# Where x is turned for the second block: TensorE transposes instead of DMA transposes, and a reordered prologue, in a linear-attention and feed-forward kernel

## The chip, the core and the metric

The kernel runs on one NeuronCore of a Trainium2 chip. The metric is the device time of one execution in microseconds (us). The core has five engines that run side by side and meet at semaphores: TensorE (PE, with its weight loads shown as PEld), VectorE (DVE), ScalarE (ACT), GpSimd (POOL) and SyncE (SP). DMAs are issued from POOL (bulk loads and stores) and from SP (a few loads, and all DMA transposes); both kinds move through the same 16 DMA engines.

## What is computed

The reference is a linear attention with cosine-weighted features, followed by a feed-forward layer with a quick GELU:

```
r = max(x, 0);  phi(x) = concat(r * cos_w, r * sin_w)        # x = q or k, weights depend on the position
kv  = einsum('bhsf,bhsd->bhfd', phi(k), v);   z = sum over s of phi(k)
att = einsum('bhsf,bhfd->bhsd', phi(q), kv) / (einsum('bhsf,bhf->bhs', phi(q), z) + 1e-6)
x   = att with heads put side by side                         # (8*576, 512)
h   = x @ w_in;  g = h * sigmoid(1.702 * h);  out = g @ w_out # w_in (512, 2048), w_out (2048, 512)
```

There are 8 batches, 8 heads, 576 positions and 64 values per head, so x has 4608 rows. All matrix products run in bf16 and accumulate in f32.

## The kernel before

**Two tilings that do not match.** Attention goes by batch: 576 rows, cut into four chunks of 128 and a tail of 64 (chunk 4). The feed-forward layer goes by blocks of `TB = 512` rows of x, nine in all. Block 1 is rows 512 to 1023: the tail of batch 0, chunks 0 to 2 of batch 1, and the first 64 rows of chunk 3 of batch 1. The tail of batch 1 (rows 1088 to 1151) is first read by block 2.

**One attention batch.** `prep` makes the features of q (`qn`) or k (`kp`) of one chunk with two DVE instructions; `prep_v` copies v into `vt`, which has a column of ones. The features of q are transposed into `qT`, by a DMA issued from SP (`turn_q`), or by eight TensorE transposes and a DVE copy (`turn_q_at`). `unit_kv` makes kv of all heads with 40 small matmuls, and two copies bring it to `kvs`. `unit_num(b, c)` multiplies a chunk with kv (8 matmuls of 65 columns into an `at` tile of PSUM) and divides on DVE: `den`, `inv`, then `xb`, the chunk of x. At last x has to be transposed into `xT`: `turn_x` does this with a DMA transpose from SP, `turn_x_at` with four TensorE transposes into an `at` tile and a copy on ACT. There are two `at` tiles, used in turn, and four `mm` tiles of one bank each.

**One block.** `mm1(i, fc)` takes 4 matmuls of 512 columns (line 249) and a GELU on ACT for each of the 16 slices of the hidden layer. `mm2` takes 64 matmuls (line 284) with `w_out` and empties the result through ACT or DVE to an output DMA. In block 0 the second product goes by parts: in slots 16 to 31 each slot does four matmuls for one of four row groups (`n % 4`), part 0 first, so that `w_out` is needed piece by piece.

**Order.** Nothing is scheduled automatically: each engine runs its instructions in the order of the program. While block `i` runs, the attention of batch `i + 1` is mixed in: the block has 32 slots, and `at(n, f, ...)` hangs a piece of work behind slot `n`. In block 0 batch 1 is worked on in slots 14 to 31: `prep` of q at 14, `turn_q_at` at 16 to 20, `prep` of k from 21, v at 24, `unit_kv` at 25, `unit_num` of chunks 0 to 4 at 26 to 30. Chunks 2 and 3 are turned by `turn_x_at` in slots 30 and 31; chunks 0, 1 and 4 by `turn_x`, whose DMA is issued from SP once DVE has written the chunk. From block 1 on all turns are DMA transposes.

**The prologue.** Batch 0 has nothing to hide behind, so it is written out by hand (lines 359 to 406): 34 matmuls on zeros while the first loads run; `prep` of k, then of q; `turn_q0`, transposes of q with a copy on ACT or DVE; `kv_half` for heads 0 to 3 and 4 to 7; `num0(n, p)` and `product0(n, p)` for half the heads and half the rows; `turn_x0(n, p)`, transposes of x into the tile `tp` with a copy on ACT. `mm1_first` does the first product of block 0 for three slices at once, in three pieces: over the first half of x's columns for all rows, then over the second half for rows 0 to 255, then for rows 256 to 511. The tail of batch 0's q is prepared last on DVE and transposed by DMA into `qT_tail` (line 404, line 189); `unit_num(0, 4)` reads it behind slot 7 of block 0. SP then issues three f32 loads of batch 1's tails, which stand behind that transpose in SP's queue.

**Loads.** POOL issues, in order, q and v of batch 0, `w_in`, the tail of q, then `w_out` and batch 1 in turn. From the ninth on each of them waits for the one eight places before it.

Of the kernel before, what the change touches and what calls it, by code (L numbers as in the profile page):

```python
# [21 lines left out]
def kernel(  # L22
# [15 lines left out]
    TB = 512  # L38
# [14 lines left out]
    def rows(c):  # L53
        return 128 if c < 4 else 64
# [4 lines left out]
    def mm_tile():  # L59
        return ps.tile([128, TB], F32, name="mm", bufs=4)  # L60
# [13 lines left out]
    def load_main(b, n, h0=0, h1=H, on=nc.gpsimd):  # L74
        if h0 == 0:
            state[b][n] = two.tile([128, 2048], BF16, name=n)
        on.dma_start(out=state[b][n][:, 256 * h0:256 * h1].rearrange("p (h e) -> p h e", h=h1 - h0),  # L77
                     in_=SRC[n][b, h0:h1, 0:512, :].rearrange("h (p c) d -> p h (c d)", c=4))
# [20 lines left out]
    def load_w_in(g, k0=0, k1=KC):  # L99
        nc.gpsimd.dma_start(out=w_in_sb[:, k0:k1, ts(g, 512)], in_=win_r[:, k0:k1, ts(g, 512)])  # L100

    def load_w_out(g):
        nc.gpsimd.dma_start(out=w_out_sb[:, ts(g, 4), :], in_=wout_r[:, ts(g, 4), :])
# [17 lines left out]
    load_tail(0, "q")  # L121
    for g in range(1, 4):
        load_w_in(g)
    load_w_out(0)
    load_main(1, "q")
    load_main(1, "k")
    load_w_out(1)
    load_main(1, "v")
# [34 lines left out]
    def part(b, n, c, h0, h1):  # L163
        if c == 4:
            return state[b][n, 4].rearrange("p (h d) -> p h d", d=D)[:, h0:h1]
        return state[b][n].rearrange("p (h c d) -> p c h d", c=4, d=D)[:, c, h0:h1]
# [5 lines left out]
    def prep(b, n, c, h0=0, h1=H, on=(nc.vector, nc.vector)):  # L172
        o = state[b]["qn"] if n == "q" else kp
        for cs, w in enumerate((cosw, sinw)):
            oc, i, wc = o[:rows(c), c, h0:h1, cs * D:cs * D + D], part(b, n, c, h0, h1), w[:rows(c), c:c + 1]
            if on[cs] is nc.scalar:
                nc.scalar.activation(oc, i, AF.Relu, scale=wc)
            else:
                nc.vector.tensor_scalar(oc, i, 0.0, wc, op0=MAX, op1=MUL)  # L179

    def prep_v(b, c, h0=0, h1=H):
        nc.vector.tensor_copy(vt[:rows(c), c, h0:h1, 0:D], part(b, "v", c, h0, h1))
# [33 lines left out]
    def kvs_half(b, n, kv, copy=nc.vector.tensor_copy):  # L216
        copy(state[b]["kvs"][:, n, :, 0:D + 1], kv[:, 0:4 * (D + 1)].rearrange("p (h e) -> p h e", h=4))  # L217
# [29 lines left out]
    def mm1_part(hps, i, fc, c0=0, c1=TB):  # L247
        for kc in range(KC):
            nc.tensor.matmul(hps[:, c0:c1], w_in_sb[:, kc, ds(fc * 128, 128)], xT[:, kc, ds(i * TB + c0, c1 - c0)],  # L249
                             start=(kc == 0), stop=(kc == KC - 1))  # L250

    def gelu(hps, fc):
        g = gpool.tile([128, TB], BF16, name="g")
        nc.scalar.activation(g, hps, AF.Gelu_apprx_sigmoid)  # L254
        gT[fc] = g

    def mm1(i, fc):
        hps = mm_tile()
        mm1_part(hps, i, fc)
        gelu(hps, fc)  # L260

    def pieces(m):
# [15 lines left out]
    def mm2(i, t, part):  # L278

        if part == 0:  # L280
            cur[t] = mm_tile()
        yps = cur[t]
        for fc in range(part * 4, part * 4 + 4):
            nc.tensor.matmul(yps, gT[fc][:, ds(t * 128, 128)], w_out_sb[:, fc, :],  # L284
                             start=(fc == 0), stop=(fc == FC - 1))
        if part == 3 and (i > 0 or t < 3):
            evac(i, t)

    def evac(i, t, on=None):
        ysb = ypool.tile([128, d_model], F32, name="ysb")  # L290
        if on is nc.vector:
            nc.vector.tensor_copy(ysb, cur[t])
        else:
            nc.scalar.copy(ysb, cur[t])  # L294
        for (p0, n, row, step) in pieces(i * 4 + t):
            nc.gpsimd.dma_start(out=out[row:row + (n - 1) * step + 1:step, :], in_=ysb[p0:p0 + n, :])  # L296
# [26 lines left out]
    def turn_q0(c, copy):  # L323
        t = mm_tile().bitcast(BF16).rearrange("p (h t) -> p h t", h=H)
        for h in range(H):
            nc.tensor.transpose(t[:, h], s0["qn"][:, c, h, :], ident)  # L326
        copy(qT[:, :, ts(c, 128)], t)  # L327

    def num0(n, p):
        nm = at_tile()  # L330
        for s in range(2):
            for h in range(4):
                nc.tensor.matmul(nm[:, s, ds(h * (D + 1), D + 1)], qT[:, 4 * n + h, ts(2 * p + s, 128)],
                                 s0["kvs"][:, n, h, 0:D + 1], start=True, stop=True)
        nm4 = nm[:, :, 0:4 * (D + 1)].rearrange("p s (h e) -> p s h e", h=4)
        den = two.tile([128, 2, 4], F32, name="den")
        nc.scalar.activation(den, nm4[:, :, :, D], AF.Identity, bias=eps)
        dens[n, p] = nm4, den

    def product0(n, p):  # L340
        nm4, den = dens[n, p]
        inv = two.tile([128, 2, 4], F32, name="inv")
        nc.vector.reciprocal(inv, den)
        nc.vector.tensor_tensor(s0["xb"][:, 2 * p:2 * p + 2, 4 * n:4 * n + 4, :], nm4[:, :, :, 0:D],  # L344
                                inv.unsqueeze(3).to_broadcast([128, 2, 4, D]), op=MUL)

    def turn_x0(n, p):
        for s in range(2):
            for j in range(2):
                nc.tensor.transpose(tp[:, p, s, j], s0["xb"][:, 2 * p + s, 4 * n + 2 * j:4 * n + 2 * j + 2, :]  # L350
                                    .rearrange("p h d -> p (h d)"), ident)
        nc.scalar.copy(xT[:, 2 * n:2 * n + 2, ds(256 * p, 256)].rearrange("p j (s t) -> p s j t", s=2), tp[:, p])

    def mm1_first(fc, kcs, c0, c1, last=False):
        for kc in kcs:
            nc.tensor.matmul(first[fc][:, c0:c1], w_in_sb[:, kc, ts(fc, 128)], xT[:, kc, c0:c1],
                             start=(kc == 0), stop=(last and kc == KC - 1))

    AC, VE = nc.scalar, nc.vector
# [2 lines left out]
    for c in range(4):  # L362
        prep(0, "k", c, on=(VE, AC))
    prep(0, "k", 4)
    prep_v(0, 4)
    for c in range(2):
        prep(0, "q", c)
        turn_q0(c, AC.copy)
    for c in range(4):
        prep_v(0, c, 0, 4)  # L370
    kv_lo = mm_tile()
    kv_half(0, 0, kv_lo)
    kvs_half(0, 0, kv_lo, AC.copy)
    prep(0, "q", 2)
    turn_q0(2, AC.copy)
    num0(0, 0)
    prep(0, "q", 3)
    for c in range(4):
        prep_v(0, c, 4, 8)
    turn_q0(3, VE.tensor_copy)  # L380
    product0(0, 0)
    kv_hi = mm_tile()
    kv_half(0, 1, kv_hi)
    kvs_half(0, 1, kv_hi, AC.copy)
# [7 lines left out]
    turn_x0(0, 1)  # L392
    num0(1, 1)
    product0(1, 1)
    for fc in range(3):
        mm1_first(fc, (0, 1), 0, TB)
    for p in range(2):
        turn_x0(1, p)
        for fc in range(3):
            mm1_first(fc, (2, 3), 256 * p, 256 * p + 256, last=(p == 1))  # L400
            if p == 1:
                gelu(first[fc], fc)
# [6 lines left out]
    for i in range(NBLK):  # L409
        work = {n: [] for n in range(32)}  # L410
        b = i + 1

        def at(n, f, *a):
            work[n].append(lambda: f(*a))

        if b < B:
            if i == 0:
                at(7, unit_num, 0, 4)
                at(7, turn_x, 0, 4)
            k0, k1, ks = (14, 25, (26, 27, 28, 29, 30)) if i == 0 else (0, 12, (17, 19, 21, 23, 25))  # L420
            at(k0, prep_new, b)
            for c in range(NC):
                at(k0, prep, b, "q", c)
                if i == 0:
                    at(k0 + 2 + c, turn_q_at, b, c)
                else:
                    at(k0 + c, turn_q, b, c)
                at(k1 - 4 + c // 2, prep, b, "k", c)
                at(k1 - 1, prep_v, b, c)
            at(k1, unit_kv, b)  # L430
            for c, k in enumerate(ks):
                at(k, unit_num, b, c)
                if i == 0 and c in (2, 3):
                    at(min(k + 2, 31), turn_x_at, b, c)
                else:
                    at(k, turn_x, b, c)
            if 0 < i and b + 1 < B:
                at(1, load_all, b + 1)
        for n in range(32):
            if n < FC:  # L440
                if i > 0 or n > 2:
                    mm1(i, n)
            elif i == 0:
                mm2(i, n % 4, (n - FC) // 4)
            elif i == NBLK - 1 and n >= 28:
                if n == 28:
                    mm2_last(i, 3)
            else:
                mm2(i, (n - FC) // 4, n % 4)
            for f in work[n]:  # L450
                f()
        if i == 0:
            evac(i, 3, nc.vector)
# [30 lines left out]
```

## Time and profile before

| quantity | value |
|---|---|
| time of the runs | median 302.47 us of 6 (301.18 to 303.97) |
| the profiled execution | 301.63 us; span 299.5 us, so 2.13 us lie outside the span |
| PE busy | 287.0 us, 96% of the span |
| DVE, ACT, POOL busy | 105.7, 119.3, 98.7 us |
| mean granted TensorE clock | 0.992 of full speed |
| 52 matmuls of the first product at the start of block 1 / of block 2, in the chain | 13.07 / 11.22 us |

The busy share says that TensorE bounds the kernel as a whole, and the stretches of the timeline say where it does not. A time is read as a start in us from the first instruction. Matmuls of 512 columns follow each other every 0.216 us (64 of them take 13.81 us in the chain of block 7), and the mean of 379 ns that a group shows for one of them is its latency, not its cost.

### The profile page before, as it was taken

What the parts mean: (1) busy time and instruction counts of PE and PEld (TensorE: products, weight loads), DVE (VectorE), ACT (ScalarE), POOL (GpSimd) and SP (SyncE); (2) the same over time, 40 slices, a digit from 0 to 9 for tenths busy, and PEclk for the clock granted to TensorE, in tenths of its full rate; (3) what the DMA queues carried; (4) which work ended last, traced back from release to release, by engine and by line L of the source; (5) the groups of instructions that cost most, each with busy time, mean ns of one, the idle gap of its engine ahead of it and who ended that gap; (6) DMA issues with size and microseconds to landing.
All of it is one profiled execution on the core that took longest, in us unless ns stands there. A gap on an engine that the chain in (4) does not pass through costs nothing.

```text
span 299.5 us, 5028 instructions
## 1 busy us (share of the span) xinstructions
PE 287.0 (96%) x1944; PEld 144.3 (48%) x1944; DVE 105.7 (35%) x349; ACT 119.3 (40%) x203; POOL 98.7 (33%) x113
## 2 busy tenths in 40 slices
PE   8869999599999999999999999999999999999994
PEld 3544456245544554455445544554455444444443
DVE  3851577921482148214831473147314200000000
ACT  4746501355116511751165116511651167127411
POOL 8542220780159114900491149003501200120021
PEclk9999999989999999999999999999999999999998
DMA  8999999999779985999699869964902510011033
GB/s 191 196 205 191 192 204 193 228 178 179 108 126 196 172 122 132 182 149 150 127 194 168 124 134 209 186 107 114 195 0 51 122 48 2 36 70 35 2 70 70
DMA packets 90935, 40.11 MB, mean 134 GB/s; under 512 B 59744, under 2 KB 88672, under 8 KB 90912
## 3 DMA queue, kind: packets, MB, share of 16 engines
q0 software_dynamic: 41312, 26.68, 59.0%
q1 hardware_dynamic: 49440, 12.98, 23.2%
q8 instruction: 15, 0.25, 0.4%
q10 hardware_dynamic: 160, 0.13, 0.2%
q14 instruction: 8, 0.07, 0.1%
HBM read 36.70 MB, written 9.44 MB: 154 GB/s over the span
## 4 chain that ended last, share of the span: by engine, by line
PE 87%; DMA 7%; DVE 2%; ACT 1%; issue 1%; SPq 0%; DVEq 0%
PE mm L249 40%; PE mm L284 39%; PE at L213 3%; PE at L233 3%; DMA vt<-in_v_dram 3%; DMA qT_tail<-qn 3%; DMA xT<-xb 2%; PE mm L308 1%; PE at L195 1%; ACT qT L327 1%; DVE xb L344 0%; PE mm L326 0%; DVE qn L179 0%; PE mm L350 0%; SPq L86 0%
## 5 line engine op out<-in xcount | busy, mean ns | idle before, releaser
L284 PE MATMUL mm<-w_out_sb,g 128*128 128x512 bf16 x560 | 129.0, 379 | 0.0
L249 PE MATMUL mm<-xT,w_in_sb 128*128 128x512 bf16 x564 | 126.0, 383 | 3.0 <-issue 3.0
L296 POOL DMA_DIRECT2D out_dram<-ysb x54 | 56.1, 1043 | 172.1 <-ACT ysb L294 170.7
L254 ACT ACTIVATE g<-mm 128x512 bf16<-128x512 f32 x144 | 85.6, 597 | 50.5 <-PE mm L249 50.0
L249 PEld LDWEIGHTS <-w_in_sb 128*128 128x128 bf16 x564 | 55.1, 99 | 68.8 <-issue 5.3
L284 PEld LDWEIGHTS <-g 128*128 128x128 bf16 x560 | 52.0, 98 | 56.6
L294 ACT COPY ysb<-mm 128x512 f32<-128x512 f32 x34 | 19.9, 586 | 112.1 <-PE mm L284 109.0
L217 DVE CAST kvs<-at 128x260 bf16<-128x260 f32 x14 | 5.4, 426 | 62.9 <-PE at L213 62.9
L241 DVE TENSOR_TENSOR xb<-at,inv 128x512 bf16<-128x512 f32 (+1 forms) x36 | 24.8, 689 | 1.2
L239 DVE TENSOR_SCALAR den<-at 128x8 f32<-128x8 f32 (+1 forms) x36 | 5.9, 165 | 52.3 <-PE at L233 52.3
L313 DVE COPY ysb<-mm 128x256 f32<-128x256 f32 x1 | 0.4, 425 | 59.4 <-PE mm L308 59.4
L233 PEld LDWEIGHTS <-qT 128*128 128x128 bf16 x280 | 13.5, 98 | 8.3 <-DVE xb L241 0.3
L233 PE MATMUL at<-kvs,qT 128*128 128x65 bf16 x280 | 14.6, 193 | 0.1
L179 DVE TENSOR_SCALAR kp<-k,cosw 128x512 bf16<-128x512 bf16 (+1 forms) x32 | 11.5, 367 | 3.8 <-DMA k<-in_k_dram 3.8
L179 DVE TENSOR_SCALAR qn<-q,cosw 128x512 bf16<-128x512 bf16 x32 | 11.4, 357 | 2.3 <-DMA q<-in_q_dram 2.3
L213 PEld LDWEIGHTS <-kp 128*128 128x128 bf16 x320 | 11.0, 97 | 1.8
L179 DVE TENSOR_SCALAR qn<-q,sinw 128x512 bf16<-128x512 bf16 x32 | 10.8, 339 | 0.0
L68 PE MATMUL mm<-warm 128*128 128x512 bf16 x34 | 9.1, 434 | 1.2 <-DVE warm L57 1.2
L213 PE MATMUL at<-vt,kp 128*128 128x65 bf16 x280 | 9.7, 193 | 0.0
L179 DVE TENSOR_SCALAR kp<-k,sinw 128x512 bf16<-128x512 bf16 x28 | 9.5, 339 | 0.0
L77 POOL DMA_DIRECT2D q<-in_q_dram x8 | 7.9, 984 | 3.4 <-DMA w_in_sb<-in_moe_w_in_dram 2.0
L77 POOL DMA_DIRECT2D v<-in_v_dram x9 | 7.9, 878 | 2.0 <-DVE qT L196 2.0
(67 smaller groups left out, 116.3 us busy)
## 6 DMA issues: line engine op xcount, KB each, us to landing
out_dram<-ysb POOLq DMA_DIRECT2D x38, 128.0 KB, 2.8
q<-in_q_dram POOLq DMA_DIRECT2D x8, 512.0 KB, 9.3
out_dram<-ysb POOLq DMA_DIRECT2D x16, 256.0 KB, 3.6
k<-in_k_dram POOLq DMA_DIRECT2D x7, 512.0 KB, 11.4
v<-in_v_dram POOLq DMA_DIRECT2D x7, 512.0 KB, 12.8
w_out_sb<-in_moe_w_out_dram POOLq DMA_DIRECT2D x4, 512.0 KB, 23.1
w_in_sb<-in_moe_w_in_dram POOLq DMA_DIRECT2D x3, 512.0 KB, 13.7
k<-in_k_dram SPq DMA_DIRECT2D x1, 1024.0 KB, 6.1
```

The costliest lines, as they stand in the source:

```text
L68: nc.tensor.matmul(wps, warm[:, 0:128], warm, start=True, stop=True)
L77: on.dma_start(out=state[b][n][:, 256 * h0:256 * h1].rearrange("p (h e) -> p h e", h=h1 - h0), in_=SRC[n][b, h0:h1, 0:512, :].rearrange("h ...
L179: nc.vector.tensor_scalar(oc, i, 0.0, wc, op0=MAX, op1=MUL)
L213: nc.tensor.matmul(kv[:, ds(h % 4 * (D + 1), D + 1)], kp[:, c, h, :], vt[:, c, h, 0:D + 1], start=(c == 0), stop=(c == NC - 1))
L233: nc.tensor.matmul(nm[:, h // 4, ds(h % 4 * (D + 1), D + 1)], q_slot(b, c)[:, h, :], state[b]["kvs"][:, h // 4, h % 4, 0:D + 1], start=Tru ...
L239: nc.vector.tensor_scalar(den[:r], nm4[:, :, :, D], 1e-6, None, op0=ADD)
L241: nc.vector.tensor_tensor(state[b]["xb"][:r, c].rearrange("p (n h) d -> p n h d", n=2), nm4[:, :, :, 0:D], inv[:r].unsqueeze(3).to_broadca ...
L249: nc.tensor.matmul(hps[:, c0:c1], w_in_sb[:, kc, ds(fc * 128, 128)], xT[:, kc, ds(i * TB + c0, c1 - c0)], start=(kc == 0), stop=(kc == KC ...
L254: nc.scalar.activation(g, hps, AF.Gelu_apprx_sigmoid)
L284: nc.tensor.matmul(yps, gT[fc][:, ds(t * 128, 128)], w_out_sb[:, fc, :], start=(fc == 0), stop=(fc == FC - 1))
L294: nc.scalar.copy(ysb, cur[t])
L296: nc.gpsimd.dma_start(out=out[row:row + (n - 1) * step + 1:step, :], in_=ysb[p0:p0 + n, :])
```

## The change

Six edits, in the order of the diff:

1. POOL issues the load of batch 1's q ahead of the first quarter of `w_out`, instead of behind it.
2. `mm1(1, 0)`, the first slice of block 1, is computed in two column ranges, 0 to 447 and 448 to 511 (448 to 511 are the rows of chunk 3).
3. In the prologue the tail of v is copied after q's first two chunks, not before them. `num0(0, 0)` comes ahead of the transposes of q's chunk 2, the features of chunks 2 and 3 come together, and `product0(0, 0)` comes ahead of the copy of chunk 3.
4. `turn_x0(1, 0)` comes ahead of the first piece of `mm1_first`, and `turn_x0(1, 1)` directly behind that piece, ahead of both pieces over the second half of x.
5. In block 0 the tail of batch 1's q is prepared at slot 22 and transposed at slot 23, not at 14 and 20.
6. In block 0 all four chunks of batch 1's x are turned by `turn_x_at`, in slots 28 to 31. The tail's `unit_num` and its `turn_x` move to slot 1 of block 1.

```diff
     for g in range(1, 4):
         load_w_in(g)
+    load_main(1, "q")
     load_w_out(0)
-    load_main(1, "q")
...
     def mm1(i, fc):
         hps = mm_tile()
-        mm1_part(hps, i, fc)
+        if (i, fc) == (1, 0):
+            mm1_part(hps, i, fc, 0, 448)
+            mm1_part(hps, i, fc, 448, TB)
+        else:
+            mm1_part(hps, i, fc)
         gelu(hps, fc)
...
     prep(0, "k", 4)
-    prep_v(0, 4)
     for c in range(2):
         prep(0, "q", c)
         turn_q0(c, AC.copy)
+    prep_v(0, 4)
...
-    prep(0, "q", 2)
-    turn_q0(2, AC.copy)
     num0(0, 0)
-    prep(0, "q", 3)
+    for c in (2, 3):
+        prep(0, "q", c)
     for c in range(4):
         prep_v(0, c, 4, 8)
+    turn_q0(2, AC.copy)
+    product0(0, 0)
     turn_q0(3, VE.tensor_copy)
-    product0(0, 0)
...
+    turn_x0(1, 0)
     for fc in range(3):
         mm1_first(fc, (0, 1), 0, TB)
+    turn_x0(1, 1)
     for p in range(2):
-        turn_x0(1, p)
         for fc in range(3):
             mm1_first(fc, (2, 3), 256 * p, 256 * p + 256, last=(p == 1))
...
-            k0, k1, ks = (14, 25, (26, 27, 28, 29, 30)) if i == 0 else (0, 12, (17, 19, 21, 23, 25))
+            k0, k1, ks = (14, 25, (26, 27, 28, 29)) if i == 0 else (0, 12, (17, 19, 21, 23, 25))
             at(k0, prep_new, b)
             for c in range(NC):
-                at(k0, prep, b, "q", c)
+                at(22 if i == 0 and c == 4 else k0, prep, b, "q", c)
                 if i == 0:
-                    at(k0 + 2 + c, turn_q_at, b, c)
+                    at(23 if c == 4 else k0 + 2 + c, turn_q_at, b, c)
...
+            if i == 1:
+                at(1, unit_num, 1, 4)
+                at(1, turn_x, 1, 4)
             for c, k in enumerate(ks):
                 at(k, unit_num, b, c)
-                if i == 0 and c in (2, 3):
+                if i == 0 and c < 4:
                     at(min(k + 2, 31), turn_x_at, b, c)
```

## The prediction

> **What bounds the kernel now.** I read the engine shares first: PE is busy 287.0 of 299.5 us, so only the stretches where PE idles or runs slowly can give time. The chain of waits shows that from block 2 to the end it is matmuls one behind the other (30.1 us a block). What can change lies before 63 us. The view of stretches around the end of block 0 (columns: PE, PEld, DVE, ACT, POOL busy, granted clock, DMA share, GB/s) shows the largest hole:
>
> ```profile
> 48.00:54.70 6.70, 6.55 (x70) 3.72 (x68) 5.46 (x17) 2.25 (x4) 1.68 (x3) 1.00 1.57 192
> 54.70:57.60 2.90, 0.00 (x0) 0.00 (x0) 2.90 (x11) 0.59 (x1) 1.96 (x1) 1.00 1.20 257
> 57.60:60.00 2.40, 2.34 (x9) 1.03 (x10) 2.40 (x11) 0.60 (x1) 2.40 (x1) 0.79 1.16 230
> 60.00:63.00 3.00, 3.00 (x9) 1.10 (x8) 1.60 (x8) 1.20 (x2) 3.00 (x3) 0.60 1.09 248
> ```
>
> PE does nothing for 2.90 us, and afterwards its clock falls to 0.79 and 0.60. The chain names the cause and prices the slow clock:
>
> ```profile
> 49.79 6.65 DMA xT<-xb
> 56.44 1.22 issue
> 57.66 13.07 PE mm L249 x52
> ...
> 89.61 11.22 PE mm L249 x52
> ```
>
> Block 1 waits for x of batch 1, which SP turns by DMA (6.65 us). The same 52 matmuls then take 13.07 us, against 11.22 in block 2: 1.85 us of slow clock. The timeline of the prologue and of block 0's slot 7 shows the second place:
>
> ```profile
> 20.26 1.30 SPq L189 DMA_TRANSPOSE qT_tail<-qn  x1
> 20.92 0.81 PE L356 MATMUL mm<-xT,w_in_sb 128*128 128x256 bf16 x6 [0.68 <-ACT xT L352]
> 22.63 0.82 PE L356 MATMUL mm<-xT,w_in_sb 128*128 128x256 bf16 x6 [0.67 <-ACT xT L352]
> 27.89 0.30 PEld L233 LDWEIGHTS <-qT_tail 128*128 128x128 bf16 x8 [0.62 <-DMA qT_tail<-qn]
> ```
>
> PE waits twice for a copy of xT (0.68, 0.67), and at 27.89 it meets the transposed tail of q at the moment it lands (20.26 + 7.59 by the chain = 27.85): the tail is just in time, with nothing to spare. The third place is DVE's queue before kv of batch 1:
>
> ```profile
> 41.70 0.42 DVE L196 COPY qT<-at 128x512 bf16<-128x512 bf16 x1 [0.51 <-PE at L195]
> 45.74 0.41 DVE L182 CAST vt<-vt 64x512 bf16<-64x512 f32 x1
> 45.93 1.53 PE L213 MATMUL at<-vt,kp 128*128 128x65 bf16 x40
> ```
>
> From 41.70 to 46.15 DVE works without a gap, and kv starts as it ends: DVE too has nothing to spare there.
>
> **Edit 6 with 2: the end of block 0.** Removed: the 2.97 us in which PE stood before block 1 (54.69 to 57.66), num of chunk 4 in slot 30 (eight matmuls move PE by 0.25: line 233 from 48.16 to 48.41) and the 0.31 it waited for its PSUM tile. Added: two more turns of four transposes (0.23 to 0.25 each; in the chain the eight of line 195 take 0.45), and waits for the two `at` tiles: num of chunk 2 now takes the tile of chunk 1, whose xb ends 50.88, and PE is there 0.25 earlier; chunk 3 about 0.1. ACT gets four xT copies of 0.59 among three evacuations of 0.59; with a slot of 1.35 us it keeps up, and the last copy ends 0.8 us after PE's last transpose. That cover is the first range of `mm1(1, 0)` (4 x 448 columns, 0.75 us); its 64-column range then waits about 0.1. Four matmuls more cost no more than 0.03 by line 233's row (31 ns for 65 columns, less the 27 ns by which each of the others got shorter). Without the split PE would wait 0.8 there. Sum before other shifts: 2.97 + 0.25 + 0.31 - 0.50 - 0.35 - 0.10 = +2.6. The tail's num returns in block 1: -0.25. Its `turn_x` on SP now stands among block 1's q transposes; chunk 2 of q waits for it behind DVE's ten q preparations (2.6 us), but is read in slot 17, some 15 us later: nothing. DVE's den, inv and xb of the tail stand ahead of batch 2's k, used in slot 12: nothing. Net +2.3.
>
> **The clock.** Without the hole the 1.85 should go too. Here the Trainium skill speaks against me. Its page "TensorE: Matmul & The Clock Gate" (What's actually happening) says that the clock halves after an idle window of about 3.4 us, and that this window runs freely, so that where it falls varies from run to run. Our hole is 2.97 us (about 3.2 between matmuls other than transposes). By the rule it should drop only sometimes: on the rule alone I would count 0 to 1.85. By the rows it did drop (0.79, 0.60), in an execution of 301.63 us; the fastest of six is 301.18, only 0.45 lower. If any had escaped the drop, it would lie near 299.8. I take 1.85 and keep 0.9 as the low end.
>
> **Edit 5: the tail of q at slots 22 and 23.** The order of DVE's instructions becomes: four qT copies, k chunks 0 to 3, q's tail, the qT copy of the tail, k's tail, v. The copy of chunk 3 ends 41.20; k's eight end at a start of 43.22 (8 x 0.262), q's tail (f32, 0.40 pitch) ends 44.09. PE reaches slot 23's transposes at 43.92 and waits 0.2. They end 44.53, DVE's copy runs 44.57 to 44.99, and k's tail, v and the cast of v's tail (2.0 us as before) end near 46.95, not 46.15. Queued behind that copy is all that kv needs. PE, at kv by 46.1, waits: its start moves by 0.87 in all. Cost -0.85 (bounds -0.3, if DVE's pitch closes up, and -1.3). The wait for the f32 tail (landing 35.04) in slot 14 goes, but was covered by PE's slot 16 (35.9): worth nothing.
>
> **Edits 3, 4, 1: the prologue.** q lands at 1.28 + 9.0 = 10.28 and DVE began on it at 10.38, so moving v's tail away gives 0.06. `num0(0, 0)` ahead of q's chunk 2 delays that chunk: its transposes start 14.15 instead of 12.99, ACT's copy (1.04) ends 15.84 instead of 14.82, DVE's copy of chunk 3, behind the product now, 16.27 instead of 15.55. `num0(0, 1)` needs both: den at 16.66 (15.94). Following it on: last xb ends near 20.2 (19.71), xT copies at 19.0, 20.1 and 21.6, and the matmuls of `mm1_first` run 19.3 to 20.6, 20.9 to 21.5, 21.65 to 22.3. Line 249 starts at 22.3 instead of 23.28: +1.0. But slot 7 follows 20 matmuls (4.32 us) later, at 26.6, and waits for q's tail. That was issued at 20.26 behind the last xb; now 20.8. With its old 7.59 it lands at 28.4: -0.5 against before. The load order helps: in the DMA view the two queues take turns, packet by packet. In 25:26, beside `w_out`, and in 27:28, beside q with its smaller packets:
>
> ```profile
> q0 software_dynamic: 171, 0.15, 91.6%
> q1 hardware_dynamic: 168, 0.04, 32.0%
> ...
> q0 software_dynamic: 245, 0.13, 90.3%
> q1 hardware_dynamic: 244, 0.06, 46.2%
> ```
>
> After the change q stands where `w_out` stood from 24.2 on. The tail's packets (about 730, starting 3.75 us after issue) at 240 a us take 3.05: landing 27.6, so +0.3. I take +0.3, bounds -0.5 and +1.0. The first quarter of `w_out` then lands where q did, about 31.75, and is needed at 35: nothing. The other quarters (38.4, 43.45, 46.05 by issue and landing) keep their places and are needed in slots 20, 24 and 28 (40.5, 44.3, 49.5). A slot 7 one us earlier would still find them.
>
> **Sum.** 2.3 + 1.85 - 0.85 + 0.3 = 3.6 us. The profiled execution would go from 301.63 to 298.0; it lies 0.84 below the median of 302.47, so I predict 298.9.
>
> **Rivals.** (a) The hole goes, and the prologue's gain reaches slot 7 (tail landing by 27, kv's wait 0.3): 3.6 + 0.7 + 0.55 = 4.85, 297.6. For it: the packet counts. Against: the later issue. Chance 0.15. (b) The hole goes but half of the clock's 1.85 was not lost in the median run, or PE idles again before the xT copies, and kv waits 1.3 and slot 7 ends 0.5 late: 3.6 - 0.95 - 0.45 - 0.8 = 1.4, 301.1; with one of them less, 300.3. Chance 0.22. (c) Slower: q's tail is the one transfer on the path. It is issued 0.5 us later in the same crowded engines, PE is there 1 us earlier, and each us of landing behind 27.85 is a us lost. If PE then idles so long that the clock falls as it did after the 2.97 us (1.85 more), the 3.3 of the rest are used up at a landing of 29.3; without the fall, at 31.15. At 31 with the fall: 1.7 us slower, 304.2. Against it: 29.3 would be a latency of 8.5 against 7.6 and 7.0 for the next transpose, and holes of 0.4 to 0.8 in the prologue left the clock at 1.00. Chance 0.08. (d) The turns do not take effect, since block 1 waits for something else that lands late, such as `xT` of batch 0's tail (29.49 + 7.0, far too early to matter): 302.5. Chance 0.03. The forecast case has 0.52.
>
> **Numbers.** The forecast's own range is 298.0 to 300.0 (the bounds of slot 7 and kv, not all at once). Over the cases 8 in 10 lie between 297.3 and 301.0; (c), (d) and the end of (b) stay out. About 0.5% (1.5 us) can be told from no change here; 300.96 is the edge. Faster by more: the forecast, (a) and over half of (b), 0.81. Same: 0.12. Slower: 0.07.
>
> **What would show it.** Right: no PE wait above 0.3 us between slot 31 and line 249 of block 1; clock 1.00 there; its first 52 matmuls near 11.3; PE waiting about 1 us for qT_tail in slot 7; PE waiting 0.7 to 0.9 for vt at kv; line 249 first at about 22.3. Wrong: a clock below 1.00 after slot 7 or at block 1; qT_tail landing past 28.4; a wait of ACT's xT copies above 0.5; line 284 waiting for `w_out` at slot 16.

## The result, and the profile after

| | median of the runs | profiled execution | its span | mean clock |
|---|---|---|---|---|
| before | 302.27 us (65 runs, 300.14 to 304.05) | 301.63 us | 299.5 us | 0.992 |
| after | 299.76 us (28 runs: one of 612.94, which nothing here explains, the others 299.13 to 301.66) | 299.67 us | 297.5 us | 0.992 |

The ratio of after to before is 0.9925, with a 95% interval of 0.9908 to 0.9943: 2.5 us less, where 3.6 were forecast. The view of stretches of the changed kernel (columns as in the prediction) shows where the hole ahead of block 1 went, and something new in the prologue:

```profile
18.00:19.70 1.70, 0.92 (x16) 0.89 (x17) 1.22 (x4) 0.76 (x2) 0.75 (x1) 0.94 1.24 207
19.70:22.80 3.10, 3.10 (x14) 1.42 (x13) 1.29 (x4) 0.59 (x1) 0.67 (x1) 0.50 1.24 206
...
49.30:57.00 7.70, 7.42 (x77) 4.24 (x74) 5.04 (x15) 3.22 (x6) 1.39 (x3) 1.00 1.32 202
57.00:60.00 3.00, 3.00 (x28) 1.62 (x26) 3.00 (x9) 1.78 (x3) 2.35 (x4) 1.00 0.54 185
60.00:63.00 3.00, 3.00 (x16) 1.34 (x15) 2.93 (x9) 2.04 (x4) 3.00 (x5) 1.00 0.95 133
```

From 57 us on PE is busy all the time at a clock of 1.00: hole and slow clock are both gone there. But from 19.7 to 22.8 us the clock is 0.50, where before it was 1.00:

```profile
20.00:22.00 2.00, 1.28 (x15) 0.97 (x13) 0.23 (x1) 0.59 (x2) 0.65 (x2) 1.00 1.24 206
```

The chain of waits of the changed kernel, in order of time:

```profile
21.12 7.80 DMA qT_tail<-qn
...
28.97 0.43 PE at L233 x8
29.40 6.91 PE mm L249 x32
...
57.14 1.81 PE mm L249 x12
58.95 0.25 PE at L233 x8
59.21 9.50 PE mm L249 x44
```

The first 13 slices of block 1 take 1.81 + 9.50 = 11.31 us, against 11.22 for the same work in block 2 and 13.07 before. No DMA of x is in the chain any more. Instead it runs through the transposed tail of batch 0's q: slot 7's `unit_num` starts at 28.97, not at 27.89. The timeline of the same execution:

```profile
19.77 2.76 PE L361 MATMUL mm<-xT,w_in_sb 128*128 128x512 bf16 x6
...
21.12 1.29 SPq L189 DMA_TRANSPOSE qT_tail<-qn  x1
...
28.97 0.43 PE L233 MATMUL at<-kvs,qT_tail 128*128 128x65 bf16 x8 [0.20 <-DMA qT_tail<-qn]
...
45.31 0.40 PE L195 MATMUL at<-ident,qn 64*128 64x64 bf16 x8 [0.31 <-DVE qn L179]
...
45.75 0.42 DVE L196 COPY qT<-at 128x512 bf16<-128x512 bf16 x1 [0.50 <-PE at L195]
...
47.69 0.41 DVE L182 CAST vt<-vt 64x512 bf16<-64x512 f32 x1
48.16 1.12 PEld L213 LDWEIGHTS <-kp 128*128 128x128 bf16 x35 [0.24 <-issue]
```

The six matmuls at line 361 (line 356 before) take 2.76 us at the low clock, instead of 1.46. The tail is issued at 21.12, not 20.26. Below, the forecast wait at kv is there: PE waits 0.31 for the tail of batch 1's q, DVE's copy waits 0.50 for PE, and kv's main part starts at 48.16, when the cast of v's tail has ended. From the start of slot 16 to the end of kv it is 36.30 to 49.40, 13.10 us; before, 35.23 to 47.46, 12.23. That is +0.87. In the chain of the kernel before:

```profile
35.23 0.86 PE mm L284 x4
...
46.09 1.36 PE at L213 x40
```

### The profile page after: what moved, and what is told of

Same layout as the page of the kernel before. It is cut to its first block, busy times and chain, and to the rows that moved or that the text cites. A ratio compares the mean times of both kernels' runs of the same rounds, so it can differ in the third digit from the quotient of the medians.

```text
span 297.5 us, 5050 instructions
## 1 busy us (share of the span) xinstructions
PE 288.6 (97%) x1956; PEld 145.3 (49%) x1956; DVE 107.4 (36%) x349; ACT 120.6 (41%) x205; POOL 92.5 (31%) x113
## 4 chain that ended last, share of the span: by engine, by line
PE 86%; DMA 6%; DVE 6%; issue 1%; ACT 0%; DVEq 0%; POOLq 0%
PE mm L249 39%; PE mm L289 38%; PE at L233 3%; DMA q<-in_q_dram 3%; PE at L213 3%; DMA qT_tail<-qn 3%; PE mm L313 1%; DVE kp L179 1%; DVE xb L349 1%; DVE qn L179 1%; DVE vt L182 1%; PE at L195 1%; DVE xb L241 1%; DVE qT L196 0%; ACT den L342 0%
## 5 line engine op out<-in xcount | busy, mean ns | idle before, releaser
L249 PE MATMUL mm<-xT,w_in_sb 128*128 128x512 bf16 (+1 forms) x568 | 124.6, 377 | 0.0
L301 POOL DMA_DIRECT2D out_dram<-ysb x54 | 50.6, 942 | 173.9 <-ACT ysb L299 173.2
L179 DVE TENSOR_SCALAR kp<-k,cosw 128x512 bf16<-128x512 bf16 (+1 forms) x32 | 12.1, 385 | 3.8 <-DMA k<-in_k_dram 3.8
L179 DVE TENSOR_SCALAR qn<-q,sinw 128x512 bf16<-128x512 bf16 x32 | 11.8, 370 | 0.0
L68 PE MATMUL mm<-warm 128*128 128x512 bf16 x34 | 9.8, 459 | 1.2 <-DVE warm L57 1.2
```

The costliest lines, as they stand in the source:

```text
L68: nc.tensor.matmul(wps, warm[:, 0:128], warm, start=True, stop=True)
```

## The experiments

All times are medians; each group ran with the kernel before on the same chip, whose medians were 302.10 to 302.21.

**1. The tail of batch 0's q, earlier.**

```diff
     num0(0, 1)
+    prep(0, "q", 4)
+    turn_q(0, 4)
     product0(0, 1)
...
-    prep(0, "q", 4)
-    turn_q(0, 4)
```

> The changed kernel with the tail of q prepared and its transpose issued ahead of product0(0, 1), in DVE's hole of 0.69 us (16.6 to 17.3), instead of behind the last product. Theory 1: issued at about 17.3, landing at about 25, slot 7 no longer waits for it; in executions without a slow clock in the prologue PE gets there at about 26.8 instead of 29.0, so 2 us less than the changed kernel; with a slow clock (as in the profile of the changed kernel, PE there at 28.8) only 0.1 less. Theory 2 (DVE's chain of products is what bounds): the 0.6 us on DVE delay product0(0, 1) and with it all that follows by up to 0.6 us, and the time is the same or up to 0.5 us longer.

Measured: 297.70 us (6 runs, 297.22 to 299.38), ratio 0.9867 (0.9818 to 0.9917). Its chain runs on PE through slot 7, where the tail had landed three us before:

```profile
22.85 0.66 PE mm L361 x6
...
23.52 0.82 PE mm L361 x6
24.34 4.32 PE mm L249 x20
28.65 0.25 PE at L233 x8
```

This profile is of an execution with the slow clock in the prologue (0.50 from 20 to 22 us) and took 299.03; the one other run with a mean clock below 0.998 took 299.38, and the four at 0.998 and more 297.22 to 297.86. So both halves of the first expectation came: 2 us when PE is in time, little (0.4 to 0.7) when it is not, if the second slow run, which has no profile, is of the same kind. What DVE lost did not show. In the changed kernel this transfer, not PE, sets the start of slot 7.

**2. Edit 3 put back** (the order of q, v and `product0` as before; edit 4 stays).

```diff
+    prep_v(0, 4)
     for c in range(2):
         prep(0, "q", c)
         turn_q0(c, AC.copy)
-    prep_v(0, 4)
...
+    prep(0, "q", 2)
+    turn_q0(2, AC.copy)
     num0(0, 0)
-    for c in (2, 3):
-        prep(0, "q", c)
+    prep(0, "q", 3)
...
-    turn_q0(2, AC.copy)
-    product0(0, 0)
     turn_q0(3, VE.tensor_copy)
+    product0(0, 0)
```

> The changed kernel with edit 3 (the order of the prologue's q, v and first product) put back. Theory 1 (slot 7 waits for the transposed tail of q, and edit 3 makes DVE issue it later): the tail's transpose is issued at 20.2 to 20.4 us instead of 21.12, lands about 28.0 instead of 28.92, and the time falls by 0.7 to 1.0 us against the changed kernel. Theory 2 (what cost the prologue its gain is the granted clock of 0.50 between 19.7 and 22.8 us, which kept PE from reaching slot 7 in time): the tail's landing does not matter, the time stays within 0.3 us of the changed kernel's, or gets worse, as PE's earlier work of edit 3 is lost.

Measured: 299.13 us (6 runs, 298.43 to 299.99), ratio 0.9895 (0.9844 to 0.9946), 0.6 less than the changed kernel. The expected issue time was missed, 21.33. With the order of before, the tail of v stands ahead of q in DVE's queue again, and in this execution its load came late:

```profile
10.87 0.67 DVE L182 CAST vt<-vt 64x512 bf16<-64x512 f32 x1 [1.13 <-DMA vt<-in_v_dram]
11.46 0.33 DVE L179 TENSOR_SCALAR qn<-q,cosw 128x512 bf16<-128x512 bf16 x1
```

q had landed at 10.3, 9.0 us after its issue at 1.28, but DVE starts on it at 11.46, against 10.38 in the kernel before and 10.52 in the changed kernel. Counted from that instruction, the issue comes after 9.87 us. With the order of before this distance is 9.87 to 9.89 in all four profiles that have it, with edit 3 it is 10.46 to 10.89 in five. So behind DVE's first q instruction edit 3 delays the tail by 0.6 to 1.0 us. Ahead of it edit 3 helps, as q no longer waits for the tail of v: the issue itself lies at 20.26 to 21.33 without edit 3 (mean 20.71) and at 21.12 to 21.26 with it (mean 21.21), 0.5 apart.

**3. Edit 1 put back** (q of batch 1 behind the first quarter of `w_out`).

> The changed kernel with q of batch 1 loaded behind the first quarter of w_out again. Theory of the prediction (q's smaller packets beside the tail let it through sooner): the tail lands 0.5 to 0.8 us later after its issue than in the changed kernel (7.8), the time rises by 0.5 to 0.8 us. Rival (q's packets have mostly gone before the tail's first packet moves, 3.9 us after the issue, so the order does not matter to the tail): within 0.2 us of the changed kernel.

Measured: 299.16 us (7 runs, 298.96 to 299.41), ratio 0.9907 (0.9872 to 0.9941). Its chain, against 7.80 us in the changed kernel:

```profile
21.24 7.11 DMA qT_tail<-qn
...
28.39 0.43 PE at L233 x8
```

The prediction's reason is reversed in this profile: without edit 1 the tail lands sooner after its issue, and the median is lower by 0.6. The DMA view shows what stood beside the tail. Of the changed kernel, in 24:25 (one queue alone) and in 27:28 (both):

```profile
q0 software_dynamic: 392, 0.20, 146.8%
...
q0 software_dynamic: 158, 0.16, 93.3%
q1 hardware_dynamic: 155, 0.04, 31.4%
```

q's small packets (392 a us) pass before the tail's first packet moves, 3.9 us after its issue; beside the tail stands `w_out`, at about 157 packets a us each. With edit 1 put back, in 27:28:

```profile
q0 software_dynamic: 250, 0.13, 92.2%
q1 hardware_dynamic: 248, 0.06, 46.2%
```

That packets alternate, and that smaller neighbours let the tail through faster, was right; that q would still be moving then was wrong. Over all profiles with the tail at its late place, landing follows issue by 7.7 to 7.9 us with edit 1 and by 7.1 to 7.9 without (mean of five 7.5), so edit 1's share is about 0.3 and not well fixed.

**4. Edits 1 and 3 both put back.**

> The changed kernel with edits 1 and 3 both put back (edit 4, which moves PE's work of the prologue, stays). Theory (the prologue's loss is two delays of the same transfer: edit 3 lets DVE issue the tail about 0.7 us later, edit 1 lets it land 0.7 us later after its issue; both only matter through slot 7): the two add up, tail landing 7.1 to 7.6 after an issue 9.9 after DVE's first q instruction, 1.0 to 1.5 us below the changed kernel, 298.3 to 298.8. Rival (they overlap, or PE gets to slot 7 too late to use it without edit 3): no better than each alone (299.13 and 299.16).

Measured: 299.03 us (6 runs, 298.52 to 299.57), ratio 0.9884 (0.9853 to 0.9915). The rival was right: no better than each alone. The tail is issued 9.89 after DVE's first q instruction (20.65), lands after 7.64 us, and slot 7 starts at 28.33, as in experiment 3 at 28.39. Edit 4 was kept in all of these. The intervals of experiments 2, 3 and 4 overlap that of the changed kernel (0.9908 to 0.9943): that undoing edit 1 or edit 3 gains some 0.6 us is likely, and for neither alone is it beyond doubt.

**5. Edits 3 and 4 alone, on the kernel before.**

> The kernel before with edits 3 and 4 (the prologue) alone. Theory 1 (DVE's issue of the tail, 0.7 us later after its first q instruction, sets slot 7): 0.4 to 0.9 us slower than the kernel before, tail issued 10.6 us after DVE's first q instruction instead of 9.88. Theory 2 (the prologue's earlier end on PE counts): faster by up to 1 us.

Measured: 301.98 us (14 runs, 300.31 to 304.23), ratio 0.9999 (0.9970 to 1.0029): neither loss nor gain to be told, and the interval leaves room for 0.9 us either way, so that theory 1's loss of 0.4 to 0.9 is not excluded. The view of waits shows what theory 1 says of the place:

```profile
PE mm L249 <- issue: 3.4, 1, 3.4
PE at L233 <- DMA qT_tail<-qn: 1.5, 1, 1.5
```

PE gets to slot 7 1.5 us too early and waits there. The issue came 10.70 after DVE's first q instruction. This run only says that no gain of the new prologue by itself can be seen.

**6. The tail of batch 1's q, behind kv.** In slot 25 behind v on DVE, its transposes in slot 31.

```diff
-                at(22 if i == 0 and c == 4 else k0, prep, b, "q", c)
-                if i == 0:
-                    at(23 if c == 4 else k0 + 2 + c, turn_q_at, b, c)
+                at(k1 if i == 0 and c == 4 else k0, prep, b, "q", c)
+                if i == 0 and c < 4:
+                    at(k0 + 2 + c, turn_q_at, b, c)
...
+            if i == 0:
+                at(31, turn_q_at, b, 4)
```

> The changed kernel with the tail of batch 1's q prepared behind v in slot 25 and transposed in slot 31, so that nothing of it stands ahead of k's tail and v on DVE. Theory 1 (edit 5 costs 0.85 us by what queues behind the tail's qT copy): PE's waits of 0.31 in slot 23 and about 0.6 inside kv go, 0.6 to 0.9 us less than the changed kernel. Theory 2 (kv waits for the load of v of batch 1, which lands near 42 us, or PE waits elsewhere later, for instance for the xT copies): within 0.2 us of the changed kernel.

Measured: 299.16 us (12 runs, 298.40 to 300.46), ratio 0.9921 (0.9889 to 0.9954). The runs fall in two heaps: seven from 298.40 to 299.43, five from 300.20 to 300.46. The profile is of one of the five (300.31):

```profile
27.00:30.00 3.00, 0.75 (x10) 0.56 (x12) 0.30 (x2) 0.59 (x1) 0.69 (x1) 1.00 1.27 189
30.00:35.00 5.00, 5.00 (x16) 1.89 (x15) 3.15 (x10) 1.99 (x4) 0.96 (x1) 0.66 1.31 190
```

In its chain kv follows slot 25 at once:

```profile
29.89 8.32 PE mm L249 x30
...
43.46 5.18 PE mm L289 x24
48.64 1.21 PE at L213 x40
```

kv's 40 matmuls take 1.21 us without a wait, so edit 5's cost is repaired. What the profiled run lost, it lost in slot 7: PE waited 2.2 us for qT_tail, the clock fell to 0.66, and 30 matmuls took 8.32 us. In experiment 2, where PE waited 1.8 us at the same place, the clock stayed at 1.00 and the same 30 took 6.64. The lower heap has a median of 298.76, 0.9 below the 299.7 of the changed kernel's 23 runs up to 300.18. That fits kv's wait, but no run of the lower heap was profiled; over all runs the medians differ by 0.6.

**7. The hole of the kernel before, filled.**

```diff
+            if i == 0:
+                at(31, fill, 12)       # 12 matmuls of 512 columns on zeros into an `at` tile
```

> The kernel before with 12 matmuls on zeros (2.6 us) into an unused PSUM tile behind the last transposes of slot 31, in the hole ahead of block 1; their result is not used. Theory 1 (the hole makes the clock fall, in some executions and not in all, and the fall costs 1.85 us): clock 1.00 behind the hole, the 52 matmuls take 11.2 us, the runs of 302 us go and the time lies near 300.3 to 300.8, where the fastest runs of the kernel before lie. Theory 2 (the clock falls for another reason, such as the load of the machine at that point, or the fall did not cost what the chain shows): 302 us as before.

Measured: 300.85 us (22 runs, 300.03 to 301.46), ratio 0.9949 (0.9929 to 0.9969), though PE still waits for x there. Its stretches, and block 1 in its chain:

```profile
54.70:57.60 2.90, 2.79 (x16) 1.30 (x15) 2.89 (x9) 0.59 (x1) 1.53 (x2) 1.00 1.09 178
57.60:60.00 2.40, 1.61 (x8) 0.61 (x7) 2.40 (x10) 0.00 (x0) 2.40 (x1) 1.00 1.14 271
60.00:63.00 3.00, 3.00 (x16) 1.36 (x14) 2.25 (x10) 2.08 (x4) 3.00 (x2) 1.00 1.12 243
...
59.00 6.63 PE mm L249 x30
...
65.69 4.70 PE mm L249 x21
```

The clock stays at 1.00, and the first 13 slices of block 1 run from 59.00 to 70.39, 11.39 us instead of 13.07. In this execution block 1 starts 1.3 us later than in the profile of the kernel before, so that its time is hardly lower; the medians of the group differ by 1.4 (302.21 and 300.85, just above the expected 300.3 to 300.8). 19 of the 22 runs have a mean clock of 0.997 or more, against 5 of the 33 runs of the kernel before in this group. No run passed 301.46, where 50 of the 65 runs of the kernel before lie at 301.5 to 304.05. The hole's price in clock is real, and it was being paid in most runs. That the runs near 300.3 are those that escaped it is read from their times; none of them was profiled.

**8. The split of `mm1(1, 0)` undone** (edit 2).

> The changed kernel with mm1(1, 0) in one column range again (edit 2 undone). Theory (the split hides the copy of chunk 3 behind 448 columns): PE waits for the copy that ends at about 57.8 in the changed kernel's profile, 0.6 to 0.8 us, and the time rises by 0.6 to 0.8 to about 300.4. Rival (the hole of 0.7 is taken by something PE would wait for anyway): within 0.2 us.

Measured: 300.57 us (11 runs, 300.09 to 302.03), ratio 0.9950 (0.9924 to 0.9976), 0.8 above the changed kernel. The view of waits on PE has the line that the changed kernel lacks:

```profile
PE mm L249 <- ACT xT L203: 0.7, 1, 0.7
```

**9. Both tails moved** (experiments 1 and 6 together).

> The changed kernel with both repairs: the tail of batch 0's q prepared and sent off ahead of product0(0, 1), and the tail of batch 1's q prepared behind v and transposed in slot 31. Theory (the two losses are separate and lie one behind the other on PE's path): the early tail's 2 us (its runs had a median of 297.7) and the 0.8 of kv's wait add up, 296.5 to 297.0. Rival (the gains overlap, because a PE that is earlier by 2 us meets a late load, w_out or v of batch 1): 297.4 to 297.9, with a wait of line 289 or of kv in the profile.

Measured: 297.55 us (6 runs, 297.25 to 297.99), ratio 0.9853 (0.9810 to 0.9897). The rival was right: hardly below experiment 1, and the new wait is the load that it named.

```profile
PE mm L289 <- DMA w_out_sb<-in_moe_w_out_dram: 0.8, 1, 0.8
```

PE is now early enough to meet the third quarter of `w_out` in slot 24.

**10. As 9, with five matmuls on zeros in PE's idle stretches of the prologue.**

> As a_both, with five matmuls of 512 columns on zeros in PE's idle stretches of the prologue (three behind num0(1, 0), two behind num0(1, 1)), into a bank that the first product overwrites; their result is not used. Theory (the clock of 0.50 at 19.7 to 22.5 us that some executions show comes from PE's idle stretches ahead of it, and costs 1.2 us now that slot 7 no longer waits): no slow clock in the prologue in any run, the runs of 298 to 299 go, median 0.2 to 0.5 below a_both and the slowest run over 1 us below that of a_both. Rival (the transposes and small matmuls of the prologue keep the clock as well as others, and what the fall depends on is where its window lies): the share of slow runs stays, and the median rises by 0 to 0.5 us, as the five matmuls push num0 and the transposes back.

Measured: 297.66 us (6 runs, 297.21 to 298.08), ratio 0.9856 (0.9816 to 0.9896): the same as 9. The clock is 1.00 throughout the prologue in this profile, as it was in that of 9. Slot 7 starts 0.2 earlier, because q landed that much earlier (DVE starts on it at 10.31, not 10.46), and the wait for `w_out` takes it back (0.9 instead of 0.8). None of these six runs has a mean clock below 0.997, and two of the six of 9 have 0.994; whether the filling prevents the fall stays open.

**11. As 9, with the third quarter of `w_out` ahead of v of batch 1.**

```diff
-    load_main(1, "v")
     load_w_out(2)
+    load_main(1, "v")
     load_w_out(3)
```

> a_both (both tails moved) with the third quarter of w_out loaded ahead of v of batch 1. Theory (line 289 waits 0.8 us for that quarter in a_both, and v is needed only 2 us later): the wait goes or moves to kv at less than half its length, 0.3 to 0.8 us below a_both's 297.55. Rival (the loads as a whole bound slot 24 and 25, both transfers are needed at about 44 us): kv's wait for v takes its place, within 0.2 us of a_both.

Measured: 296.86 us (6 runs, 296.58 to 297.26), ratio 0.9813 (0.9786 to 0.9840). This is the best version: 5.3 us below the kernel before of its own group, 2.9 below the changed kernel's median. Its chain goes through the load of v and on through DVE to kv:

```profile
19.24 24.47 DMA v<-in_v_dram
...
43.73 1.24 DVE vt L182 x5
...
45.01 1.25 PE at L213 x36
```

So a load of the first 44 us is now what the chain to block 1 passes through. DVE stands still for it only 0.30 us, so that little is left to gain by an earlier v alone.

## Why the prediction was right or wrong

The direction and the main mechanism held; the sum was 1.1 us too high by the medians, and one term of it, the prologue's, accounts for about that much.

- **End of block 0 (edits 6 and 2), right.** From the start of slot 16 to the start of block 2 it is 54.38 us before (35.23 to 89.61) and 51.29 after (36.30 to 87.59): 3.09 less. The terms for hole, clock and kv gave 2.3 + 1.85 - 0.85 = 3.3. Measured are 1.76 for the clock (13.07 to 11.31) and -0.87 for kv, which leaves 2.2 for the hole. The two waits for an `at` tile's xb came out at 0.31 each (0.35 were set down for both). Experiment 8 confirms the cover that was named for the last copy, 0.8 us.
- **The clock, right in size, with a false reason.** Experiment 7 shows that the fall is caused by the idle PE. It does not come in every run: of the 65 runs of the kernel before 14 lie from 300.14 to 300.73, about 2.0 below the median, and the other 51 from 301.18 up. The Trainium skill's rule that was weighed ("TensorE: Matmul & The Clock Gate", What's actually happening: the window runs freely) fits that share. Its 3.4 us does not: an idle window of that length has no room in a hole of 2.97 us, and the clock fell to 0.79 and 0.60 behind it all the same; here the measurement decides. That none of the first six runs had escaped was taken as a sign that the fall comes always; they were six from the larger share, which was luck. The median still paid it.
- **Edit 5, right.** +0.87 measured, 0.85 set down, by the queue that was named. Experiment 6 removes it.
- **The prologue, wrong.** This is the failed step: "landing 27.6, so +0.3". In the two profiles slot 7 starts 1.08 later, not 0.3 earlier. Part of that is chance: with the order and the loads of before it starts at 27.89, 28.33 and 28.55 (the kernel before, experiments 4 and 7), with edits 1 and 3 at 28.97, 28.98 and 29.19 (the changed kernel, experiments 8 and 6), 0.8 later in the mean, and -0.8 in place of +0.3 is the 1.1 that the sum misses. Two parts of the step failed. The landing was put at 3.75 + 3.05 = 6.8 us after the issue, because q would stand beside the tail; q had passed by then, the landing took 7.8, and over the profiles edit 1 delays it by about 0.3 instead of speeding it up. And the issue came at 21.12, not 20.8; of the 0.3 between, about 0.2 is q landing later in that execution. What was right is PE's own part (line 249 starts at 22.5 to 22.8 in five profiles with a full clock, 22.3 was set down), that PE's earlier end in the prologue brings nothing, and that the tail is the transfer that decides: experiment 1.
- **The granted clock in the prologue, not foreseen.** The changed kernel's profile shows 0.50 from 19.7 to 22.8, so that line 249 starts at 24.29, not 22.3. It cost almost nothing, because slot 7 waits for the tail anyway: PE waited 0.20 there, against 1.8 in the profile of experiment 8, whose prologue ran at 1.00; both start slot 7 at 29.0. The five executions of the changed kernel with a mean clock of 0.991 or 0.992 took 299.23 to 299.94, no longer than the others.
- **Rival (c).** Its mechanism exists (experiment 6: a wait of 2.2 us in slot 7, then a clock of 0.66), but the landing stayed near 29, where it does not eat up the gain. Four of the 28 runs of the changed kernel lie at 300.96 to 301.66 with a mean clock of 0.994. They fit this mechanism, but none of them was profiled.

## What to carry to other kernels

Before counting an earlier engine as a gain, look for the next transfer it will meet: here a DMA that had been just in time swallowed the prologue's gain, and once it was moved, a weight load came next. A piece that nobody needs soon (the tail of q) should stand in its queue behind everything that is needed soon. When an idle stretch makes the clock fall in some runs and not in others, the spread of the runs hints at its price, and a few runs are not enough to say how often it is paid.

## What the runs showed of the hardware

- Idle PE and the clock: holes of 2.97 and 3.4 us (the kernel before and experiment 5) were followed by a fall (0.79 and 0.77 in the next 2 to 3 us), in slot 7 a wait of 2.2 us was (0.66 over 5 us) and one of 1.8 us was not (1.00). In the prologue the clock fell to 0.50 in two profiles (the changed kernel and experiment 1) although no wait of PE behind its first matmuls was longer than about 1.0 us, and stayed at 1.00 in other profiles with the same waits (experiment 8). What decides there stays open.
- At the head of the prologue the load of q of batch 0, issued at 1.28 us in every kernel, landed 9.0 to 9.5 us later in the 13 profiles, and that of the tail of v, issued at 2.06, 7.5 to 8.8 us later. A spread of 0.5 and 1.3 us from one execution to the next is as large as what most edits to the prologue are worth, so single profiles of it have to be compared with care.
